# A table that fixes the whole order, and a short way for chunk 0's attention output, in a one-core adaLN transformer block

## The chip, the cores and the metric

One core of one Trainium2 chip runs the whole kernel in one launch. The metric is the device time of one execution in microseconds (us). Before the change it is 331.8 us, the median of three runs (331.46 to 332.3).

The engines are named as in the profile: PE is TensorE (matrix products, PEld its weight loads), DVE is VectorE, ACT is ScalarE, POOL is GpSimd. SP computes nothing and issues most of the DMA transfers, one after the other; a few are issued from ACT's queue. Each engine runs its own list of instructions strictly in the listed order, and an instruction that waits for a semaphore holds up everything listed behind it on that engine.

## The reference

```python
mod = (silu(c) @ w_mod)                       # six rows of 640: sa, ca, ga, sb, cb, gb
h = layernorm(x) * (1 + ca) + sa
x = x + ga * A(h)                             # A: attention, 32 heads of 20, sliding window of 256
h = layernorm(x) * (1 + cb) + sb
x = x + gb * B(h)                             # B: (sigmoid(h @ w_gate) * (h @ w_up)) @ w_down
# A(h): q, k, v = split(h @ wqkv);  o = softmax(mask(q k^T / sqrt(20))) v;  return o @ wo
```

x has 2048 rows of 640, wqkv is 640 x 1920, wo is 640 x 640, w_gate and w_up are 640 x 1536, w_down is 1536 x 640 and w_mod is 640 x 3840. Everything is bf16 outside PSUM.

## The kernel before

**Tiling.** The 2048 rows are cut into eight chunks of 256 (two blocks of 128 rows). For each chunk `a` the stages are: load of x, LayerNorm 1 (`ln_stats` on DVE, the power on POOL, the normalised rows `xh` on DVE or POOL), a turn to columns giving `hT`, the projections to q, k and v (`qkv`), a turn of q and k to `QT` and `KT`, scores (`score_set`), exponentials on ACT, masks on POOL, the product with v (`burst`), the division by the row sum (`norm`), the output projection with `wo` and the residual (`outproj`), LayerNorm 2, a turn giving `h2T`, and the gated MLP (`mlp`). The weights `wqkv`, `wo`, `wg`, `wu`, `wd` are loaded once and stay on chip. The gate rows ga and gb are multiplied into `wo` and `wd` ("wos", "wds" below) once they are computed in `mod_rows`, which sends them through a small DRAM buffer to all partitions (`gbc`).

**Two ways of turning.** The rows of chunks 0 to 2 (`NPH = 3`) and the q and k of chunks 0 and 1 (`NPQ = 2`) are turned on PE by products with `ident`, then copied out of PSUM. The later ones, and every `h2T`, are turned by DMA transposes issued on SP; `h2T` and the DMA-turned `hT` are then scaled and shifted in place (`modulate`).

**The way out of attention.** `norm` leaves `On`, a tile of 128 partitions holding four heads, each padded from 20 to 32 rows. Eight DMAs per chunk ("doc", 40 KB each) write the 20 used rows of each head to DRAM, and two DMAs read them back without the gaps as `oT`, five tiles of 128 rows, so that the output projection needs five passes (`NDT = 5`) per 128 x 320 result. For chunk 0 these DMAs are issued from ACT's queue (`OWE`), for the others from SP.

**Buffers that bound the order.** PSUM products use four banks in rotation (pool `M`); scores have one tile of four banks (`S`). Q and k that are turned by DMA pass through four staging buffers (`stg`), two per block of rows, which come free when the transposes have read them. Raw and normalised x of later chunks use four buffers (`x0`).

**What sets the order.** Nothing runs in the order in which it is written. `Prog.op` records each operation with its engines, a planner's cost, its dependences and its buffers; `schedule` is a list scheduler that walks time forward on those costs, and among the operations that could start next takes the one with the smallest priority from the table `PRIO` (line 408 on); `emit` then writes each engine's list with the semaphore waits. DMA transfers rotate over 24 semaphores, and each also waits for the one before it on the same semaphore.

**Lines of the profile.** Products are recorded by one helper, so all of full height have line 722 and those on parts of the array (scores, the product with v, the modulation rows) line 723; L703 and L714 are filler products that only keep PE running at the start; L880, L881 copy `hT` out, L916 and L917 copy the projections and turned tiles out, L1038 is the exponential, L1063 the mask, L1105 to L1114 `norm`, L1187 the residual, L847 and L848 `modulate`, L839 the DMA transposes, L623 and L624 all other DMAs.

Of the kernel before, what the change touches and what calls it, by code (L numbers as in the profile page):

```python
# [8 lines left out]
ALU = mybir.AluOpType  # L9
# [72 lines left out]
class Prog:  # L82
# [8 lines left out]
    def op(self, eng, fn, dur, reads=(), writes=(), prio=50.0, lat=0.05, work=None, tmin=0.0, extra=(), tag="", hold=(),  # L91
# [13 lines left out]
        o.prio = PRIO[self.seq] if self.seq < len(PRIO) else prio  # L105
# [46 lines left out]
    def schedule(self):  # L152
        free = {e: START for e in ENGS}
        bw = 0.0
        lastturn = False
        cand = {e: {} for e in ENGS}
# [6 lines left out]

        def arm(o):
            t = o.tmin
            for d in o.deps:
                t = max(t, d.end + (0.0 if (d.eng == "pe" and o.engs == ("pe",)) else d.lat))
            o.ready = t
            for e in o.engs:
                cand[e][o.seq] = o  # L170

        def slot_time(pool, s):
            ten = pool.tenant[s]
            if ten is None:
                if not all(x.done for x in pool.init[s]):
                    return None
                return max([x.end + x.lat for x in pool.init[s]], default=0.0)
            if ten.left:
                return None
            return max(x.end + x.lat for x in ten.rel)  # L180

        def slots_for(o):

            st = 0.0
            taken = {}
            got = []
            for t in o.tiles:
                if t.slot is None and t.mate is not None:
                    if any(g[0] is t for g in got):
                        continue  # L190
                    bs = None
                    for s in range(0, len(t.pool.tenant), 2):
                        ra, rb = slot_time(t.pool, s), slot_time(t.pool, s + 1)
                        if ra is not None and rb is not None and (bs is None or max(ra, rb) < bs[0]):
                            bs = (max(ra, rb), s)
                    if bs is None:
                        return None
                    got += [(t, bs[1] + t.odd), (t.mate, bs[1] + 1 - t.odd)]
                    st = max(st, bs[0])
                elif t.slot is None:  # L200
                    bs = None
                    used = taken.setdefault(t.pool, set())
                    for s in range(len(t.pool.tenant)):
                        if s in used:
                            continue
                        rt = slot_time(t.pool, s)
                        if rt is not None and (bs is None or rt < bs[0]):
                            bs = (rt, s)
                    if bs is None:
                        return None  # L210
                    used.add(bs[1])
                    got.append((t, bs[1]))
                    st = max(st, bs[0])
                else:
                    for x in t.prev:
                        st = max(st, x.end + x.lat)
            return st, got

        for o in self.ops:
            if o.nleft == 0:  # L220
                arm(o)
        n = len(self.ops)
        placed = 0
        while placed < n:
            best = None
            for e in ENGS:
                c = cand[e]
                if not c:
                    continue
                lst = []  # L230
                tmin = None
                for o in c.values():
                    st = max(free[e] + (SWITCH if e == "pe" and o.mode != pemode else 0.0), o.ready)
                    if e == "dve" and o.port:
                        st = max(st, free["pool"])
                    elif e == "pool":
                        st = max(st, portend)
                    if o.isdma and e == "sp":
                        st = max(st, bw - QMAX)
                    if o.tiles:  # L240
                        got = slots_for(o)
                        if got is None:
                            continue
                        st = max(st, got[0])
                    lst.append((st, o))
                    if tmin is None or st < tmin:
                        tmin = st
                if not lst:
                    continue
                eps = PE_EPS if e == "pe" else 0.04  # L250
                pick = min((x for x in lst if x[0] <= tmin + eps), key=lambda x: (x[1].prio, x[1].seq))
                key = pick[0]
                if e == "dve" and pick[1].port:
                    key = max(max(free[e], pick[1].ready) + PORTLAG, pick[0])
                if best is None or key < best[0]:
                    best = (key, e, pick[1], pick[0])
            if best is None:
                left = [(o.tag, o.engs, [t.pool.name for t in o.tiles if t.slot is None]) for e in ENGS
                        for o in cand[e].values()][:40]
                raise RuntimeError(f"no op can be placed: {placed} of {n}: {left}")  # L260
            _, e, o, st = best
            for x in o.engs:
                cand[x].pop(o.seq, None)
            o.eng = e
            for t, s in slots_for(o)[1]:
                ten = t.pool.tenant[s]
                t.prev = list(t.pool.init[s]) if ten is None else list(ten.rel)
                t.slot = s
                t.pool.tenant[s] = t
# [26 lines left out]
            placed += 1  # L296
# [12 lines left out]
            for x in o.succ:  # L309
                x.nleft -= 1  # L310
                if x.nleft == 0:
                    arm(x)
# [90 lines left out]
def c_pe(n):  # L403
# [128 lines left out]
LEAD = 2  # L532
# [14 lines left out]
def build(nc, A_x, A_wqkv, A_wo, B_x, B_w_gate, B_w_up, B_w_down, c, w_mod, out, S=2048):  # L547
# [131 lines left out]
    for i in range(4):  # L679
        load_w3(320 * i, 320 * i + 320, 1.12, 0.30 + 0.005 * i, "wq" if i < 2 else "wk", lat=-0.4)  # L680
# [648 lines left out]
```

## Time and profile before

| what | value |
|---|---|
| median of three runs | 331.8 us |
| the profiled execution, whole | 332.45 us |
| its span, first to last instruction | 330.7 us |
| mean granted TensorE clock | 0.995 |
| PE, DVE, ACT, POOL busy | 319.8, 213.3, 214.2, 186.9 us |
| products on PE | 4918 |
| bytes moved by DMA | 37.87 MB, mean 114 GB/s |

The span and the 1.75 us around it make up the profiled execution's time. Busy time of PE counts from the start of a product to its modelled end, so it includes the filler products at the start and products that ran at a lower clock.

Some durations that the steps need, each the mean of one instruction: a copy of 128 x 512 out of PSUM is 0.69 us on DVE and 0.60 us on ACT; the exponential of 128 x 1536 is 1.45 us; a mask of 128 x 1024 is 1.06 us on POOL; `norm` of half a chunk is two transposes of 0.69 us, a reciprocal of 0.35 us, a product of 0.83 us and a transpose of 1.23 us; the issue of one DMA transpose holds SP 1.24 us in quiet stretches and up to 4.4 us in busy ones.

### The profile page before, as it was taken

What the parts mean: (1) busy time and instruction counts of PE and PEld (TensorE: products, weight loads), DVE (VectorE), ACT (ScalarE), POOL (GpSimd) and SP (SyncE); (2) the same over time, 40 slices, a digit from 0 to 9 for tenths busy, and PEclk for the clock granted to TensorE, in tenths of its full rate; (3) what the DMA queues carried; (4) which work ended last, traced back from release to release, by engine and by line L of the source; (5) the groups of instructions that cost most, each with busy time, mean ns of one, the idle gap of its engine ahead of it and who ended that gap; (6) DMA issues with size and microseconds to landing.
All of it is one profiled execution on the core that took longest, in us unless ns stands there. A gap on an engine that the chain in (4) does not pass through costs nothing.

```text
span 330.7 us, 11708 instructions
## 1 busy us (share of the span) xinstructions
PE 319.8 (97%) x4918; PEld 224.0 (68%) x4918; DVE 213.3 (65%) x419; ACT 214.2 (65%) x319; POOL 186.9 (57%) x271
## 2 busy tenths in 40 slices
PE   7999888979999999999999999999999999999997
PEld 2664633535786658765777557877787788788885
DVE  5688888768979673676395748657645577273232
ACT  1598786788688687948787977794878673112120
POOL 3127868878898786657566847493747493011000
PEclk9999999979999999999999999999999999999999
DMA  7999799995523639205712484610411323202101
GB/s 267 374 363 350 121 327 264 165 231 94 107 68 76 113 88 151 60 18 96 137 23 59 85 119 76 117 46 5 116 44 24 97 48 36 65 22 42 42 0 42
DMA packets 71695, 37.87 MB, mean 114 GB/s; under 512 B 45274, under 2 KB 70362, under 8 KB 71642
## 3 DMA queue, kind: packets, MB, share of 16 engines
q1 hardware_dynamic: 67792, 33.67, 46.1%
q10 hardware_dynamic: 3850, 3.44, 3.3%
q8 instruction: 39, 0.64, 0.8%
q14 instruction: 14, 0.11, 0.1%
HBM read 21.30 MB, written 5.25 MB: 80 GB/s over the span
## 4 chain that ended last, share of the span: by engine, by line
PE 91%; DMA 4%; DVE 1%; ACT 1%; POOL 1%; issue 1%; ACTq 0%; POOLq 0%
PE M L722 74%; PE S L723 8%; PE M L723 7%; DMA QT<-stg 2%; PE S L703 2%; DMA hT<-x 1%; ACT E L1038 1%; PE S L722 0%; POOL E L1063 0%; DVE QT L917 0%; ACT hT L880 0%; POOL st L819 0%; DVE silubc L694 0%; PE S L714 0%; ACT hT L847 0%
## 5 line engine op out<-in xcount | busy, mean ns | idle before, releaser
L1038 ACT ACTIVATE E<-S 128x512 bf16<-128x512 f32 (+2 forms) x184 | 151.1, 878 | 44.6 <-PE S L723 42.4
L1063 POOL TENSOR_SCALAR_AFFINE_SELECT E<-E 128x512 bf16<-128x512 bf16 (+1 forms) x176 | 142.8, 837 | 62.4 <-ACT E L1038 61.6
L722 PE MATMUL M<-wqkv,hT 128*128 128x480 bf16 (+1 forms) x340 | 73.9, 361 | 3.6 <-DMA QT<-stg 1.2
L722 PE MATMUL M<-h2T,wu 128*128 128x256 bf16 x480 | 65.7, 273 | 0.0
L722 PE MATMUL M<-h2T,wg 128*128 128x256 bf16 x480 | 62.8, 273 | 0.0
L722 PE MATMUL M<-wd,hh 128*128 128x320 bf16 (+2 forms) x396 | 57.9, 295 | 0.0
L1232 ACT ACTIVATE sig<-M 128x512 f32<-128x512 f32 x48 | 28.8, 604 | 40.0 <-PE M L722 36.8
L1234 DVE SCALAR_TENSOR_TENSOR hh<-sig,M 128x512 bf16<-128x512 f32 x48 | 32.5, 678 | 32.5 <-PE M L722 16.0
L722 PEld LDWEIGHTS M<-wqkv,hT 128*128 128x128 bf16 x340 | 31.1, 99 | 32.6 <-issue 2.3
L722 PEld LDWEIGHTS M<-h2T,wg 128*128 128x128 bf16 x480 | 46.1, 98 | 7.4 <-issue 0.3
L722 PEld LDWEIGHTS M<-h2T,wu 128*128 128x128 bf16 x480 | 45.4, 98 | 7.9 <-issue 0.2
L722 PEld LDWEIGHTS M<-wd,hh 128*128 128x128 bf16 x396 | 37.1, 98 | 13.4
L1105 DVE STREAM_TRANSPOSE T<-M 128x512 f32<-128x512 f32 x32 | 21.2, 698 | 23.1 <-PE S L723 21.0
L723 PEld LDWEIGHTS S<-QT,KT 20*64 20x64 bf16 (+1 forms) x1856 | 19.9, 100 | 21.2 <-ACT E L1038 11.9
L723 PE MATMUL S<-QT,KT 20*64 20x256 bf16 (+5 forms) x1856 | 32.1, 228 | 1.5 <-ACT E L1038 1.0
L1253 DVE TENSOR_TENSOR x<-M,x 128x320 bf16<-128x320 f32 (+2 forms) x33 | 15.8, 477 | 26.7 <-PE M L722 26.4
L812 DVE BATCH_NORM_STATS2 st<-x 128x6 f32<-128x320 bf16 x64 | 28.3, 477 | 3.3 <-DMA x<-in_A_x_dram 3.1
L817 POOL TENSOR_SCALAR st<-st 128x2 f32<-128x2 f32 x16 | 4.5, 280 | 38.8 <-DVE st L814 38.5
L722 PE MATMUL M<-wo,oT 128*128 128x320 bf16 x160 | 25.0, 300 | 0.0
L723 PE MATMUL M<-E,V 128*32 128x128 bf16 (+1 forms) x960 | 22.7, 246 | 0.8 <-DVE hT L881 0.6
L917 DVE CAST stg<-M 128x480 bf16<-128x480 f32 (+1 forms) x25 | 14.6, 584 | 13.3 <-PE M L722 12.7
L723 PEld LDWEIGHTS M<-E,V 128*32 128x32 bf16 x960 | 19.2, 97 | 5.2 <-issue 4.4
(75 smaller groups left out, 252.5 us busy)
## 6 DMA issues: line engine op xcount, KB each, us to landing
x<-in_A_x_dram SPq DMA_DIRECT2D x17, 160.0 KB
doc<-On SPq DMA_DIRECT2D x56, 40.0 KB
wd<-in_w_mod_dram SPq DMA_DIRECT2D x6, 320.0 KB
wd<-in_B_w_down_dram SPq DMA_DIRECT2D x4, 480.0 KB
wqkv<-in_A_wqkv_dram SPq DMA_DIRECT2D x4, 400.0 KB
wu<-in_w_mod_dram SPq DMA_DIRECT2D x5, 320.0 KB
x<-in_A_x_dram ACTq DMA_DIRECT2D x9, 160.0 KB
oT<-doc SPq DMA_DIRECT2D x7, 192.0 KB
```

The source lines that it names most:

```text
L703: ins = e.matmul(p_S.aps[0][:, 3, :], Eall[:, 0, 0:128], Eall[:, 0, 128:640], start=True, stop=True)
L722: return e.matmul(o, l, r, start=st, stop=sp, skip_group_check=True)
L723: return e.matmul(o, l, r, start=st, stop=sp, tile_position=tp, skip_group_check=True)
L812: A("dve", lambda e, g, bi=bi, j=j: e.bn_stats(v(bi * 12 + j * 6, 6), src[bi].ap[:, j * 320:(j + 1) * 320]), 0.48, reads=[src[bi].r()], wr ...
L817: A("pool", lambda e, g: e.tensor_scalar(v(28, n), var(), EPS, None, op0=ALU.add), 0.2, reads=[st.r(("m", bi)) for bi in range(n)], writes ...
L917: return e.tensor_copy(dst(), src())
L1038: A("act", lambda e, eng: e.activation(dst(), src(), ACT.Exp, scale=SM_SCALE), c_act(n), reads=[Sp.r()], writes=[E.r(key)], prio=3, tag=f" ...
L1063: A("pool", lambda e, eng: e.affine_select(rows(dst), rows(src), pattern=[[0, 8], [sign, n]], compare_op=ALU.is_ge, fill=0.0, base=base, c ...
L1105: A("dve", lambda e, g, h=h: e.transpose(T1.ap[:, 512 * h:512 * h + 512], X[h].ap), 0.694, reads=[X[h].r()], writes=[T1.r(h)], prio=3.5, t ...
L1232: A("act", lambda e, g, pg=pg, sg=sg: e.activation(sg.ap[:], pg.ap[:], ACT.Tanh, scale=0.5), c_act(512), reads=[pg.r()], writes=[sg.r()], ...
L1234: A("dve", lambda e, g, pu=pu, sg=sg, f0=f0: e.scalar_tensor_tensor(out=hh.ap[:, f0:f0 + 2, :], in0=sg.ap[:].rearrange("p (a b) -> p a b", ...
L1253: A("dve", lambda e, g, ps=ps, bi=bi, c0=c0, n=n: e.tensor_tensor(x1[bi].ap[:, c0:c0 + n], ps.ap[:, 0:n], x1[bi].ap[:, c0:c0 + n], op=ALU. ...
```

## The change

**Order.** The list scheduler is gone. The table `PRIO` now has one number for each operation: operations are taken in the order of these numbers, and the number modulo 5 names the engine that runs it. Buffers are still given out by the planner's clock. Several planner costs and latencies are changed with it.

**Chunk 0's way out of attention.** Chunk 0 no longer goes through DRAM. `wo` is loaded a second time as `wop`, spread so that it matches the padded heads: 20 rows of weights, then 12 rows of zeros, for each of four heads, in eight tiles (`NG = 8`). `wop` lies in the memory of `hh` (so two of the modulation loads move from there to `wd`), is cleared by one DVE operation and filled by four DMAs of 20 partitions. The projection of chunk 0 multiplies `On` by `wop` directly, in eight passes instead of five. As `wop` has no gate in it, a DVE operation multiplies each product by `gbc` into a `sig` tile, and a second operation (on DVE or POOL) adds the residual. `wo` is gated for the later chunks as before. The MLP's gate row gets a tile of its own (`gbd`).

**Chunk 0's LN2 output** is turned on PE (`NPB = 1`), with scale and shift in the copies out of PSUM, in place of two DMA transposes and `modulate`.

**Loads.** `wm2`, `wo` and others have other places in SP's list; most x loads of the middle stage move from ACT's queue to SP's. By the built programs ACT's queue issues 8 DMAs where it issued 28, SP's 183 transfers and transposes become 195, and PE's list has 4940 products.

```diff
-        o.prio = PRIO[self.seq] if self.seq < len(PRIO) else prio
+        o.prio = PRIO[self.seq] if PRIO else prio
...
+        for o in sorted(self.ops, key=lambda x: x.prio):
+            assert all(d.done for d in o.deps), o.tag
+            e = ENGS[o.prio % 5]
+            assert e in o.engs, (o.tag, e)
+            o.eng = e
+            st = max([o.tmin, free[e] + (SWITCH if e == "pe" and o.mode != pemode else 0.0)]
+                     + [d.end + (0.0 if d.eng == "pe" and e == "pe" else d.lat) for d in o.deps])
...
-NPB = 0
+NPB = 1
...
-    gbc = sb("gbc", [128, D])
+    gbc, gbd = sb("gbc", [128, D]), sb("gbd", [128, D])
...
-             hhall[:, NDT * D:2 * NDT * D].rearrange("p (t f) -> p t f", t=NDT),
+             wd[:].rearrange("p a b -> p (a b)")[:, NDT * D:2 * NDT * D].rearrange("p (t f) -> p t f", t=NDT),
...
-    dma(lambda: wo[:], lambda: A_wo.rearrange("(t p) f -> p t f", p=128), 2.25, writes=[R_wo], prio=0.5, tag="wo")
-    load_bulk(wm_ap[2], wm_src[:, :, 2560:3200], Rm[2], 0.46, 0.6, "wm2", cuts=(3, 5))
+    R_wop = [R(f"wop{j}") for j in range(4)]
+    wop = hhall[:, 0:NG * D].rearrange("p (g f) -> p g f", g=NG)
+    o_wz = A(("dve", "pool"), lambda e, g: e.memset(hhall[:, 0:NG * D], 0.0), {"dve": 1.6, "pool": 4.7}, writes=R_wop, prio=1)
+    for j in range(4):
+        dma(lambda j=j: wop[32 * j:32 * j + DH], lambda j=j: A_wo.rearrange("(g j r) f -> j r g f", j=4, r=DH)[j], 0.56,
+            writes=[R_wop[j]], prio=0.5 + 0.01 * j, tag="wop", nonc=True)
...
         def close(q, X):
             On = Tile(p_On, f"On{a}_{q}")
             norm(X, On, a)
+            if not a:
+                Ons.append(On)
+                if q == 1:
+                    x1, h2 = outproj(a, Ons)
+                    mlp(a, x1, h2)
+                return
...
+                if not a:
+                    pairs = [(lambda t=t, bi=bi, half=half, ps=ps: (
+                        ps.ap[:, 0:320], oT[t // 4].ap[:, t % 4 * CH + bi * 128:t % 4 * CH + bi * 128 + 128], wop[:, t, half * 320:half * 320 + 320]))
+                        for t in range(NG)]
+                    o = pe_chain(ps, 320, pairs, [[oT[t // 4].r()] + R_wop for t in range(NG)], 15, f"wo{a}",
+                                 hold=[x1[bi]], gate=NG - 1, step=4)
...
+                    A("dve", lambda e, g, ps=ps, sg=sg, half=half: e.tensor_tensor(
+                        sg.ap[:, 0:320], ps.ap[:, 0:320], gbc[:, half * 320:half * 320 + 320], op=ALU.mult), c_dve(320),
+                      reads=[ps.r(), R_gbc], writes=[sg.r()], prio=4.5, tag="gate_0")
+                    A(("dve", "pool"), lambda e, g, sg=sg, bi=bi, half=half: e.tensor_tensor(
+                        x1[bi].ap[:, half * 320:half * 320 + 320], sg.ap[:, 0:320], x1[bi].ap[:, half * 320:half * 320 + 320],
+                        op=ALU.add), {"dve": c_dve(320), "pool": 0.56}, reads=[sg.r(), x1[bi].r()], writes=[x1[bi].r(("h", half))], prio=4.5, port=True, tag="res1_0")
+                    continue
```

More of the change, by code (lines that the diff above doesn't have):

```diff
@@ L162, in schedule @@
         portend = 0.0
[L164 to L170, printed above, removed]
+        freed = {}
         def slot_time(pool, s):
@@ L177, in slot_time @@
                 return max([x.end + x.lat for x in pool.init[s]], default=0.0)
[L178 to L186, printed above, removed]
-            for t in o.tiles:
[L188 to L269, printed above, removed]
@@ L308, in schedule @@
                     t.rel = list(last.values())
[L309 to L312, printed above, removed]
+                    freed[t] = max(x.end + x.lat for x in t.rel)
         self.order = order
@@ L809, in v, with part @@
             return st.ap[:, lo:lo + w]
+        def part(bi, j):
+            return [src[bi].r(("h", j))] if ("h", j) in src[bi].res else []
         for bi in range(n):
@@ L874, in pe_transposes @@
         prev = {}
-        for blocks, (dt, pv, rp) in [((bi,), x) for bi in range(2) for x in evs] if a == 0 else [((0, 1), x) for x in evs]:
+        for blocks, (dt, pv, rp) in [((bi,), x) for bi in range(2) for x in evs] if a == 0 and ln == "a" else [((0, 1), x) for x in evs]:
             lo, hi = blocks[0] * 128, blocks[-1] * 128 + 128
```

75 lines of the change are left out of this document (53 added, 22 removed), and 223 rows, old and new, of the table PRIO.

## The prediction

> **What bounds the kernel now.** I read the page's totals first, then PE in stretches, then PE's waits, then PE's timeline.
>
> ```profile
> PE 319.8 (97%) x4918; PEld 224.0 (68%) x4918; DVE 213.3 (65%) x419; ACT 214.2 (65%) x319; POOL 186.9 (57%) x271
> ...
> DMA  7999799995523639205712484610411323202101
> ```
>
> PE is busy for 97% of the span, so two things can shorten the kernel: fewer or faster products, and the 3% in which PE stands. DMA is near full for the first nine of 40 slices, so a load cannot be made earlier there without another becoming later.
>
> ```profile
> 0.00:10.00 10.00, 7.44 (x55) 1.00 0.83 284
> ...
> 30.00:40.00 10.00, 9.44 (x198) 1.00 0.84 201
> 40.00:50.00 10.00, 8.41 (x122) 1.00 1.20 288
> 50.00:60.00 10.00, 8.77 (x115) 1.00 1.08 255
> 60.00:70.00 10.00, 8.95 (x203) 1.00 0.99 190
> 70.00:80.00 10.00, 8.91 (x136) 0.83 0.85 162
> 80.00:90.00 10.00, 10.00 (x140) 1.00 0.54 91
> ```
>
> The columns are stretch, length, PE busy (products), granted clock, DMA share, GB/s. PE has no gap from 80 us until the end's tail. What can be won lies before 80 us: between 30 and 80 us PE is busy 44.48 of 50 us, so 5.52 us idle.
>
> ```profile
> PE M L722 <- DMA QT<-stg: 1.2, 1, 1.2
> PE M L722 <- ACT hT L847: 1.1, 1, 1.1
> PE S L723 <- ACT E L1038: 1.0, 1, 1.0
> PE M L722 <- DVE stg L917: 0.9, 1, 0.9
> PE M L723 <- DVE hT L881: 0.6, 1, 0.6
> PE S L723 <- DVE QT L917: 0.6, 1, 0.6
> ```
>
> No single cause: DMA transposes (QT; hT before its scaling), the exponential and copies out of PSUM each hold PE once. In common they have that PE's list at that place holds only projections of chunks 2 to 4, which share the staging buffers and the transposes; chunk 0's MLP (wg, wu) begins at 82.8 us, since its input goes through DRAM and two DMA transposes.
>
> ```profile
> 1.30 5.18 PE L703 MATMUL S<-E 128*128 128x512 bf16 x12 [1.30 <-DVE E L698]
> 6.41 0.17 PE L688 MATMUL M<-ident,oT 5*128 5x5 bf16 x1
> ...
> 8.52 0.45 PE L722 MATMUL S<-silubc,wd 128*128 128x64 bf16 x10 [1.26 <-DVE st L814]
> ...
> 12.29 2.20 PE L722 MATMUL M<-wqkv,hT 128*128 128x320 bf16 x15 [0.30 <-ACT hT L880]
> ...
> 71.07 3.87 PE L722 MATMUL M<-wqkv,hT 128*128 128x480 bf16 x10 [1.14 <-ACT hT L847]
> ...
> 75.23 2.20 PE L722 MATMUL M<-wqkv,hT 128*128 128x480 bf16 x10
> ```
>
> Two further losses. At 71.07 ten products take 3.87 us that take 2.20 us at 75.23: 1.67 us at a lower clock (0.83 in that stretch) after waits of 0.98 and 1.14 us within 2.6 us. And the start is a chain of waiting: the small product that turns c (L688) stands behind twelve fillers of 0.43 us, and from it follow silu(c), the modulation products at 8.52 and the first projection at 12.29 us.
>
> **The change, part by part.** The sum is made on the profiled execution, 332.45 us (span 330.7 and 1.75 around it), 0.65 above the median.
>
> *Start: -1.4 us.* In the new list the turning of c stands behind eight fillers: 1.30 + 8 x 0.43 = 4.74 instead of 6.41 us. DVE then has three LN statistics from 3.94 us (0.42 each), c, a fourth, silu, two aggregates (0.2 each) and the broadcast of 0.80 us: about 7.1 instead of 8.37 us. The six fillers left end near 7.1 too, so the modulation products start at about 7.25, 1.3 us earlier, and have one filler of 0.22 us less between them: 1.4 in all. The loads bear it: five loads of w_mod and two of x, 1.97 MB, stand ahead, and at the first slice's rate (267 GB/s over 8.3 us, 2.2 MB) they are in by 7.6 us; the first wqkv pieces follow. The added clearing of wop on DVE costs nothing where DVE waited for x, from 1.45 to 3.94 us: by the rows of the clearings (0.33 us for 320 elements, 0.21 for 192) 2560 elements are 2.4 us. Without that cover up to all 1.4 us go. Three clearings of staging buffers move to POOL, which stood idle 4.66 us before its first LN power at 8.58. Bounds: 0 (c lands only after 6.4 us, which the trace hides) to 2.0.
>
> *Added products: +2.2 us.* Eight passes instead of five for four results are 12 products of 128x320, at 0.137 us start to start (15 in 2.05 us): 1.64. Ten turns of LN2 rows at 0.058 us (four in 0.23): 0.58. Both are on PE's path. Upper bound from busy time by count: 12 x 0.156 (25.0 us / 160) + 10 x 0.114 (3.2 / 28) = 3.0. [...]
>
> *Middle stage: -7.2 us (5.52 idle and 1.67 of clock), and new waits of +2.5.* Eight doc transfers, two oT loads and two h2T transposes of chunk 0 go; a wop of 0.8 MB comes (2.3 us of DMA at 350 GB/s, issued by 35 us, mostly before the stage). ACT's queue issues 20 DMAs fewer; at 0.28 to 0.46 us each some ten of them lay between 35 and 55 us, among its exponentials. With chunk 0's MLP ready sooner, PE's list has it about 40 projection products (8.5 us) earlier, interleaved with chunk 4's projections, and V projections that need no staging buffer lie between q and k. So every wait listed above has other work in its place.
>
> What is late next: adding PE's new list up (0.213 us per 480 columns, 0.137 per 320, 0.36 per score set, 0.8 and 1.44 for products with v), from a first projection at 10.9 us, chunk 0's projection comes at 10.9 + 38.8 = 49.7 us. It needs the second half of `norm`, whose product with v ends at 42.3. DVE has statistics of chunks 4 and 5 listed ahead of it, and these wait for x loads that SP now issues behind two hT transposes. Before, those x loads were issued at 39.9 to 41.6 us and DVE got them at 44.5 and 47.5. SP passes the two transposes at 38.98 before; the loads that gate them are free some 3 us earlier now, so I put the last x load's issue at 38 and its landing at 43 to 44.5; norm and what DVE has between (a V copy 0.66, wos 0.9, gq and modt 0.65) take 4.9 + 2.2 us: 50 to 51.6, up to 2 us late. Behind that wait stand all of PE's products. Then gate (0.48), add (0.48 on DVE, 0.54 to 0.88 on POOL by its nearest rows), statistics, power (1.0), xh and copies (0.55 each) lie between chunk 0's last projection at 56.8 and its MLP at 64.3: they fill 6 to 7.5 us, 0 to 0.7 late. I take 2.5 for both and small others. Bounds: 0.5, and 7.2 if the stage idles as before. The gate and LN2 work on DVE (four products more, copies in place of in-place scaling) is otherwise hidden: DVE is busy 8 us in 10 there.
>
> [...] In this trace 2.1 us in two pieces cost 1.67 us, and 1.19 us at 55 us nothing; by the costlier row 1.7 us would be added.
>
> *After 80 us: 0.* No wait before; every product stays. Up to +1.5 if the new order waits where the old did not. The tail keeps its form (a last piece of 192 columns instead of 128: +0.1).
>
> Sum: 332.45 - 1.4 + 2.2 - 7.2 + 2.5 = 328.55; less 0.65 for the median, 327.9, say 328.0.
>
> **The rivals.**
>
> *All waits go* (new waits 0.5): 326.0. For it: each part has work in its place. Against: the norm chain above has no slack. Chance 0.15.
>
> *The stage idles as before* (new waits 5 to 7): 330.4 to 332.4, about 331.5. For it: DMA stays full until 80 us with no fewer bytes, and the transposes take their 4 to 8 us whatever the order. Against: the staged projections lie further apart. Chance 0.17.
>
> *Slower: the x loads come late enough to stop norm.* If SP passes the two hT transposes no earlier than now (39 us), the last x load lands at about 47, norm ends at 54, chunk 0's projection waits 4.3 us; meanwhile the two PSUM banks of its product with v stay taken, so that the V projections of chunk 3 wait too; MLP 0 shifts as well (1.5) and the clock falls (1.7): 7.5 us and no gain at the start: 331.8 + 2.2 - 7.2 + 7.5 = 334.3 with 0, 332.9 with the start's 1.4. It decides once norm's input stage on DVE (L1105's successor) starts after 46 us. For it: DVE waited 0.25 and 0.96 us for just these loads. Against: their gates come earlier. Chance 0.15.
>
> That the order changes nothing is excluded: the list has the eight-pass products and no doc transfer of chunk 0.
>
> **How the numbers follow.** Forecast 0.53 (328.0, own range 325.8 to 330.3), rivals 0.15, 0.17, 0.15. A measurement of this kernel can tell about 0.3% (1 us) from no change. Faster than 330.8: 0.53 and 0.15, and a quarter of the third case, 0.04: 0.72. Within 330.8 to 332.8: most of the rest of the third, 0.12. Slower: 0.16. The range of 8 in 10 runs from 325.0 to 333.2: it leaves out the tail of the first rival and most of the slower one beyond.
>
> **What would show it.** The first projection near 10.9 us instead of 12.29; PE idle between 30 and 80 us near 2.5 us instead of 5.5, its clock 1.00 in every stretch; MLP 0 (wg) from about 65 to 68 us instead of 82.8; the largest PE wait just before the products of On with wop, released by DVE; x landing on DVE before 45 us. Wrong if PE waits for DMA as long as before, if a gap appears after 80 us, or if the first projection is not earlier.

## The result, and the profile after

| | before | after |
|---|---|---|
| median of runs (lowest to highest) | 331.88 us (331.46 to 332.3) | 337.02 us (335.52 to 339.63) |
| ratio, with its 95% interval | | 1.0149 [1.0109, 1.0188] |
| profiled execution, whole / span | 332.45 / 330.7 us | 335.52 / 333.8 us |
| first projection, first MLP product | 12.29, 82.8 us | 11.52, 73.9 us |
| PE idle from 30 to 80 us | 5.52 us | 5.09 us |
| mean granted clock | 0.995 (profiled execution) | 0.985 to 0.995, run by run |

The changed kernel is 1.5% slower. Here and below, a run more than 1.5% above the fastest of its kernel is left out of the ratio (two of again's ten, one of xslot's four, three of wopearly's twelve), while medians and ranges count every run. In the page of after the totals differ little:

```profile
PE 322.5 (97%) x4939; PEld 225.2 (67%) x4940; DVE 207.9 (62%) x412; ACT 219.2 (66%) x328; POOL 183.3 (55%) x274
```

PE in stretches (start and end, length, PE busy, products, granted clock, DMA share, GB/s) shows where the expected gain is not:

```profile
0.00:10.00 10.00, 7.42 (x69) 1.00 0.80 256
...
30.00:40.00 10.00, 8.90 (x149) 1.00 1.15 245
40.00:50.00 10.00, 8.51 (x153) 1.00 0.89 227
50.00:60.00 10.00, 9.93 (x156) 1.00 0.97 215
60.00:70.00 10.00, 7.68 (x171) 1.00 1.10 255
70.00:80.00 10.00, 9.89 (x110) 0.83 0.92 196
80.00:90.00 10.00, 10.00 (x176) 1.00 0.55 148
```

From 30 to 80 us PE still stands 1.10 + 1.49 + 0.07 + 2.32 + 0.11 = 5.09 us, and one stretch has the clock of 0.83 again. The waits are other ones (wait, total us, times, longest):

```profile
PE S L671 <- issue: 1.9, 1, 1.9
PE M L670 <- DVE T L1058: 1.5, 1, 1.5
PE S L651 <- DVE E L646: 1.3, 1, 1.3
PE S L670 <- DVE x L785: 1.2, 1, 1.2
PE M L671 <- DMA wu<-in_w_mod_dram: 0.9, 1, 0.9
```

Two of them are the case: one of 1.5 us for T, which is `norm`'s first step, and one of 1.9 us that the profile puts down to nothing ("issue"). PE's timeline (start, length, operation, count, in brackets the idle time before it) has them at 49.20 and 69.95 us:

```profile
49.20 0.58 PE L670 MATMUL M<-wqkv,hT 128*128 128x480 bf16 x2 [1.48 <-DVE T L1058]
...
67.64 0.38 PE L671 MATMUL S<-QT,KT 20*128 20x64 bf16 x28 [0.29 <-ACT E L991]
69.95 0.21 PE L671 MATMUL S<-QT,KT 20*128 20x64 bf16 x4 [1.93 <-issue]
```

The first is a V projection that needs the PSUM bank in which the product with v waits for `norm`. The second stands in the middle of a set of 32 equal products, between the 28th and the 29th, where no operand can be missing.

The chain of work that ended last (start, length, what) leads back from the first of them:

```profile
32.01 7.45 DMA hT<-x
...
39.53 0.33 SPq L568
...
40.38 4.99 DMA x<-in_A_x_dram
45.39 1.28 DVE st L765 x3
...
48.52 0.63 DVE T L1058
```

SP issues chunk 3's two transposes of x at 32.01 us. The next x tile in SP's list goes into a buffer which these transposes still read; SP therefore stands until they have landed, at 39.5 us. The three x loads follow at 39.53, 40.38 and 41.30, and DVE has statistics of chunks 4 and 5 ahead of `norm`: it starts T at 48.44 us.

### The profile page after: what moved, and what is told of

Same layout as the page of the kernel before. It is cut to its first block, busy times and chain, and to the rows that moved or that the text cites. A ratio compares the mean times of both kernels' runs of the same rounds, so it can differ in the third digit from the quotient of the medians.

```text
span 333.8 us, 11744 instructions
## 1 busy us (share of the span) xinstructions
PE 322.5 (97%) x4939; PEld 225.2 (67%) x4940; DVE 207.9 (62%) x412; ACT 219.2 (66%) x328; POOL 183.3 (55%) x274
## 4 chain that ended last, share of the span: by engine, by line
PE 82%; DMA 6%; SPq 3%; ACT 3%; POOL 2%; issue 2%; DVE 1%; POOLq 0%; ACTq 0%
PE M L670 69%; PE S L671 8%; PE M L671 6%; SPq L568 3%; DMA wqkv<-in_A_wqkv_dram 2%; ACT E L991 2%; DMA hT<-x 2%; DMA x<-in_A_x_dram 1%; POOL E L1016 1%; DVE st L765 1%; ACT hT L800 1%; POOL st L772 0%; POOL x L782 0%; DVE stg L870 0%; DVE T L1058 0%
## 5 line engine op out<-in xcount | busy, mean ns | idle before, releaser
L1016 POOL TENSOR_SCALAR_AFFINE_SELECT E<-E 128x512 bf16<-128x512 bf16 (+1 forms) x176 | 141.0, 829 | 68.8 <-ACT E L991 63.8
L670 PE MATMUL M<-wqkv,hT 128*128 128x480 bf16 (+1 forms) x340 | 75.8, 358 | 2.0 <-DVE T L1058 1.5
L670 PE MATMUL M<-h2T,wu 128*128 128x256 bf16 x480 | 70.6, 273 | 0.0
L670 PE MATMUL M<-h2T,wg 128*128 128x256 bf16 x480 | 67.5, 273 | 0.0
L670 PE MATMUL M<-wo,oT 128*128 128x320 bf16 x140 | 23.1, 300 | 0.0
L1067 DVE STREAM_TRANSPOSE On<-Tn 128x1024 bf16<-128x1024 bf16 x16 | 19.7, 1232 | 0.2
```

Source lines behind the costliest of these rows:

```text
L670: return e.matmul(o, l, r, start=st, stop=sp, skip_group_check=True)
L1016: A("pool", lambda e, eng: e.affine_select(rows(dst), rows(src), pattern=[[0, 8], [sign, n]], compare_op=ALU.is_ge, fill=0.0, base=base, c ...
L1067: A("dve", lambda e, g: e.transpose(On.ap[:], Tn.ap[:]), 1.22, reads=[Tn.r()], writes=[On.r()], prio=4, tag=f"tr2_{a}")
```

## Experiments

Whole lists would be long, so an edit of the order is shown as the engine's list with names: `x8` to `x11` are loads of x (128 rows each), `wg0`, `wu1` and so on the first and later parts of those weights, `wop` one of the four transfers of the spread copy, `T3` chunk 3's transposes of x. Ratios are to the kernel before, run on the same chip beside them. The runs are spread over several chips; kernels of different chips, wide and after among them, are compared by these ratios alone.

### The changed kernel again, and the first explanation: the x loads and norm

> The changed kernel as it is, a second profile of it. Theory A (late tiles of x): the statistics of chunks 4 and 5 hold VectorE again, the second norm of chunk 0 starts at 48 us or later and TensorE waits 1.2 to 1.8 us for its first transposes. Theory B (instruction supply): the gap of 1.93 us that no semaphore explains need not come back at the same place; if it is TensorE waiting for its own instructions it should appear here too, somewhere between 60 and 75 us, with one instruction packet late beside it. If the gap is absent and the time is still above 334 us, B explains little. Time 335 to 339 us by both.

Measured: 337.28 us (334.09 to 341.12), 1.0126 [1.0086, 1.0165]. The wait for T (1.6 us) and the gap behind the 28th of 32 products (1.6) are there again; idle from 30 to 80 us is 5.26 us. So neither is a chance of one execution.

```diff
 x9 gets the buffer that chunk 2's rows have left; SP:
-T3 wg0 x9 wop x8 wu0 x11
+T3 wg0 x8 x9 wop wu0 x11
```

> Tile 9 of x goes into the buffer that chunk 2's turned rows left, and is issued behind tile 8, so SP no longer stands until the transposes of chunk 3 have landed (it stood from 36.2 to 39.5 us). Theory A: tiles 8 and 9 are issued at 37 to 38 us and land by 43.5, VectorE waits under 0.5 us for x, the second norm of chunk 0 starts by 47, TensorE's wait of 1.48 us for it goes to under 0.4, and the time falls by 1.5 to 3 us. Theory B: the time moves by less than 1 us unless the unexplained gap of 1.9 us goes by chance. Rival C (the transfer queues are full anyway): the tiles land as late as before, 44.5 to 45.5, whatever the issue time, and nothing changes.

Measured: 338.13 us, 1.0124 [1.0049, 1.0198]. The first x load is issued at 36.09 us instead of 39.5, but DVE gets its data only at 43.76 us (after: 44.35), norm starts at 47.36 and PE waits 1.9 us for T. SP's stand was a symptom: issued 3.4 us earlier, the load was used only 0.6 us sooner.

```diff
 DVE:
-statistics of chunks 4 and 5 ... norm (second half of chunk 0)
+norm (second half of chunk 0) ... statistics of chunks 4 and 5
```

> On VectorE the second norm of chunk 0 (two input transposes, reciprocal, division, output transpose, with the one small modulation add they need) goes ahead of the statistics of chunks 4 and 5. All else is as in the changed kernel. Theory A: the input transposes start as soon as the product with v is done, at 45.5 to 46 us instead of 48.4, the wait of 1.48 us on TensorE goes, the first projection of chunk 0 starts by 52 instead of 54.7, and the time falls by 1.5 to 3 us. If the statistics are late instead, the transposes of chunk 4 and its projections pay: a new TensorE wait behind 75 us of up to 2 us. Theory B: the gap of 1.9 us near 68 us stays and with it most of the loss.

> Both edits together. Theory A: as the better of the two alone, 333 to 334.5 us, no more, because they remove one and the same wait. Theory B: what is left above 332 us is the unexplained gap and the low clock behind it, about 3.5 us together where it occurs.

Measured: 337.65 us, 1.0156 [1.0075, 1.0237], and with both edits 338.76 us, 1.0176 [1.0122, 1.023]. The waits of PE in the first:

```profile
PE M L829 <- DVE V L1029: 3.3, 1, 3.3
PE S L830 <- ACT E L1150: 1.9, 3, 1.4
PE M L830 <- POOL E L1175: 1.8, 2, 1.2
...
PE S L830 <- issue: 0.2, 1, 0.2
```

No wait for T is left, and the time is no better: the copy of V out of PSUM, the exponentials and POOL's masks hold PE instead. The copy of V is late by the edit itself, since DVE now has the statistics ahead of it. The masks stand on POOL behind the scaling of chunk 3's `hT`, which needs the same transposes; these land later still here, and the scaling starts at 41.89 us instead of 40.21. The exponentials are late because one x load is left in ACT's own queue: it is issued at 41.79 us, and ACT computes nothing for 3.12 us around it. So the test is not a clean one, but taking the wait for T away gained nothing, and the late transposes stand ahead of two of the three new waits.

### What lies ahead of the transposes

The added loads are the suspect. The next kernel keeps the order and takes the bytes of the copy away (64 columns of one row are left of each transfer), so that chunk 0's output projection multiplies almost only by zeros:

```diff
-wop[32 * j:32 * j + DH], A_wo.rearrange("(g j r) f -> j r g f", j=4, r=DH)[j]
+wop[32 * j:32 * j + 1, 0, 0:64], A_wo.rearrange("(g j r) f -> j r g f", j=4, r=DH)[j, 0:1, 0, 0:64]
```

> The four loads of the second copy of w_o (0.8 MB) shrink to 64 columns of one row each, so chunk 0's projection is left out in effect (its products run on zeros); every instruction stays. Theory C (transfers of the stage up to 80 us are the bound, and the copy adds to them): tiles 8 and 9 of x land 1.5 to 3 us earlier, the wait for the second norm shrinks from 1.5 us to under 0.6, the w_mod wait at 37 us goes, and the time falls by 2 to 3 us. Theory A (only SP's standing order matters): under 1 us, since x is issued as late as before. Theory B: the unexplained gap of 1.6 to 1.9 us behind the 28th of 32 score products stays.

Measured: 333.01 us (332.01 to 333.95), 1.0027 [0.9999, 1.0055]. The x load behind the transposes is issued at 36.25 us, and the wait for T is gone. But two gaps of the other kind stand there:

```profile
50.41 0.58 PE L670 MATMUL M<-wqkv,hT 128*128 128x480 bf16 x2 [1.18 <-issue]
68.09 0.24 PE L671 MATMUL S<-QT,KT 20*128 20x64 bf16 x4 [2.49 <-issue]
```

So most of the loss comes from the copy's loads, and the gap has another cause.

```diff
 SP:
-T3 wg0 x9 wop x8 wu0 x11 gate wg0
+T3 x8 x9 wop x11 gate wg0 wg0 wu0
```

> Behind chunk 3's transposes SP issues tiles 8, 9 and 11 of x and the last quarter of the copy first, and only then the halves of w_gate and w_up (1.7 MB) that stood ahead of them; tile 9 takes the buffer that chunk 2 left. Moving the issue alone by 3.4 us brought the landing only 1.6 us forward (43.8 instead of 45.4), because 0.58 MB of w_gate was ahead in the queue. Theory C: x lands by 41.5, the statistics of chunks 4 and 5 are done before the product with v is (45.5), TensorE's wait for the second norm goes to under 0.3 us and the time falls by 1.5 to 2.5 us, unless w_gate or w_up is now late at 74 us. Theory B: the gap near 68 us stays.

Measured: 335.57 us, 1.011 [1.005, 1.017]. The transposes land still later, at about 41.5 us; the wait for T goes, but waits for exponentials (2.2 us), a modulation load at the start (1.9), masks (1.2) and two gaps (1.9, 1.2) come. Here too ACT stands at its x load:

```profile
41.42 0.37 ACTq L726 DMA_DIRECT2D x<-in_A_x_dram  x1
41.85 0.60 ACT L1149 ACTIVATE E<-S 128x512 bf16<-128x512 f32 x1 [2.69 <-issue]
```

This change of places, behind the transposes, is no cure.

### The gap in the middle of equal products

The page of after has 39 packets of 16 KB in a queue named "instruction":

```profile
q8 instruction: 39, 0.64, 0.8%
```

PE's products and weight loads are 4939 + 4940 instructions, 253 to a packet; by this count alone the author took the packets for blocks of PE's own instructions. The transfers in short windows show such a packet at 53.9 us and the next only at 67.6 us, 13.7 us later; in the kernel before, the packets between 16 and 86 us come 6 to 11 us apart. (One earlier interval in after is as long, 26.8 to 41.1 us, and leaves no gap.) From 61.2 to 63.3 us SP issues four loads of weights, 1.7 MB. The theory: PE's next block of instructions stands behind them.

The traces show this beside it. Such gaps stand in after, again, xslot, norm, nowop, nowspread, xfirst, woback, wobspread3 and wide, 13 in all, from 0.2 us (norm) to 2.6 (woback). In the timelines of after, again, nowop, nowspread and wide they stand at only two places of PE's list, behind the 28th of the 32 products and inside the V projection shown for nowop. Between the two lie 252 products (nowop), with their weight loads 504 instructions or, at 253 each, two packets. In after PE goes on 2.3 us after a packet has started (67.6 and 69.95 us), in wide 2.5 us (63.84 and 66.33). Two edits test what makes the packet late; one moves two of the loads, the other cuts five filler products at the start into 19 pieces, so that by the theory a block ends 14 products earlier.

```diff
 SP:
-... wd wg1 wd wu1 ... q and k transposes of chunk 3
+... wd wd ... q and k transposes of chunk 3, wg1 wu1
```

> Two of the four bulk loads that SP issues in one burst at 61 to 63 us (0.77 MB of w_gate and w_up, first needed near 85 us) go behind the four query and key transposes of chunk 3. Theory B (TensorE waits for a block of its own instructions, which stands in the transfer engines behind the burst): the block comes earlier and the gap behind the 28th product shrinks from 1.6-1.9 us to under 0.7; with it the low clock that can follow it; 1 to 3 us off the time. If the gap is not from transfers it stays at 1.6 to 1.9 us.

Measured: 334.64 us (333.21 to 336.15), 1.0068 [1.0043, 1.0093]. The gap is gone, the packet comes at 65.8 us, and the wait for T (1.8 us) stays.

```profile
68.68 0.41 PE L829 MATMUL S<-QT,KT 20*128 20x64 bf16 x32 [0.29 <-ACT E L1149]
```

```diff
-ins = e.matmul(p_S.aps[0][:, 3, :], Eall[:, 0, 0:128], Eall[:, 0, 128:640], start=True, stop=True)
+cut = (0, 512) if k or i > 4 else (0, 128, 256, 512) if i == 4 else (0, 128, 256, 384, 512)
+for a, b in zip(cut, cut[1:]):
+    ins = e.matmul(p_S.aps[0][:, 3, a:b], Eall[:, 0, 0:128], Eall[:, 0, 128 + a:128 + b], start=True, stop=True)
```

> Five warm-up products at the start are cut into 19 pieces with the same columns in all: 14 products more, 28 instructions, no work added. Theory B: if the gap is TensorE at the end of a fetched block of instructions, it moves with the count and comes behind the 14th of the 32 score products instead of the 28th, 1.5 to 2 us long as before. If it hangs on the data or on a buffer it stays behind the 28th. Time as the changed kernel, 335 to 339 us.

Measured: 335.06 us (333.79 to 336.88), 1.0081 [1.0051, 1.011].

```profile
68.80 0.41 PE L673 MATMUL S<-QT,KT 20*128 20x64 bf16 x32 [1.23 <-ACT E L993]
```

The gap does not move to the 14th product, as was expected: it is gone, the packet comes at 62.0 us, ahead of the loads' bulk, and waits for exponentials (2.2 us in all) come instead. So the gap goes when loads are moved (spread), and also when 14 products are added at the start with no load moved (shift). When PE asks for a packet no trace shows. In shift the packet started with 132 products to go to the place of the gap, in spread with 62, in after with 28. That the loads hold it up fits, but is not shown: each edit also shifts other waits, and the gap's size follows from no formula here.

### Both causes removed

```diff
 SP's list of spread, with this too:
-wop[32 * j:32 * j + DH], A_wo.rearrange("(g j r) f -> j r g f", j=4, r=DH)[j]
+wop[32 * j:32 * j + 1, 0, 0:64], A_wo.rearrange("(g j r) f -> j r g f", j=4, r=DH)[j, 0:1, 0, 0:64]
```

> Two edits that were run alone, together: the second copy of w_o is not loaded (chunk 0's projection left out in effect, every instruction kept), and the 0.77 MB of w_gate and w_up go behind chunk 3's transposes. Theory B+C (the loss is transfers: the added copy, and blocks of TensorE's instructions that stand behind bulk loads): the gap of 2.5 us that was left near 68 us goes too; 330 to 331.5 us, the time at which the prediction's sum would arrive without the new waits. If the sum itself was wrong (the added products and turns cost far more than 2.2 us), the time stays at 332.5 to 333.5.

Measured: 331.08 us (329.46 to 332.24), 0.9977 [0.9948, 1.0006], with the clock at 1.0 in all ten runs. PE in stretches:

```profile
30.00:40.00 10.00, 9.78 (x152) 1.00 0.94 253
40.00:50.00 10.00, 8.82 (x185) 1.00 0.88 190
50.00:60.00 10.00, 9.97 (x125) 1.00 0.99 181
60.00:70.00 10.00, 8.60 (x182) 1.00 1.25 235
70.00:80.00 10.00, 10.00 (x117) 1.00 0.93 252
```

Idle from 30 to 80 us is 2.83 us, near the 2.5 us that the prediction gave as the mark of success; the first projection starts at 10.85 us (forecast 10.9), and MLP 0 at 68.81 us (forecast 65 to 68). Without the copy's bytes and with these loads moved, the order does what the forecast pictured, but the time is still 3 us above it. Two gaps that the profile puts down to "issue" are left, 1.21 and 0.57 us.

### Bytes, or the form of the transfers

If it is the bytes, moving others of the same number should do as well. First the load of `wo` (0.82 MB), issued at 13.1 us in after, was put later, with one part of `wg1` moved too; then with all of `wg1` and a part of `wu1` behind the transposes; then with the edits of xslot and shift on top:

```diff
 SP (wolate; wospread has the lower line in place of the upper one's second part):
-... wo ... last load of wm1 ... wg1 ... x11 ... q and k transposes of chunk 3
+... last load of wm1, wo ... x11 wg1 ... q and k transposes of chunk 3
+... last load of wm1, wo ... x11 ... q and k transposes of chunk 3, wg1 wg1 wu1
```

> Nothing left out. The first copy of w_o (0.8 MB, needed from 51 us) is issued behind w_mod's last piece of the gate instead of ahead of the copy, and 0.58 MB of w_gate (needed at 85 us) behind tile 11 of x instead of at 23 us. Theory C: w_mod's piece lands before TensorE asks for it (wait of 0.5 to 0.9 us at 37 gone), the tiles of x up to 11 are not delayed by those 1.4 MB, and 0.5 to 2 us are won, less than the 4.2 us that came from not loading the copy at all, since the bytes stay. Theory A: no change over 0.5 us. Theory B: the gap near 68 us stays or grows.

> Nothing left out. w_o's first copy later as in the run with it alone, and three bulk loads (1.34 MB of w_gate and w_up, needed from 85 us) behind chunk 3's transposes. Theory B+C: both gains, 332.5 to 334.5 us; if the three loads now hold up the tiles of x of chunks 6 and 7 behind them, a wait shows on VectorE at 85 to 95 us.

> The run before it with two edits more: tile 9 of x in the buffer that chunk 2 left, issued behind tile 8, and 14 products more from cutting five warm-up products, which moves the ends of the instruction blocks by 28 instructions. Theory B+C: 332 to 334 us; the wait for the second norm under 1 us and no unexplained gap over 0.7 us before 80 us. By the prediction's sum nothing under 330 is to be had.

Measured: 337.9 us, 1.0184 [1.0117, 1.0252]; 335.13 us, 1.0109 [1.0062, 1.0157]; 338.42 us, 1.0198 [1.0149, 1.0246]. All missed. In the first the transposes land later still, at about 42.4 us, ACT's x load waits for them, and exponentials hold PE for 4.8 us in all. Then `wo` was moved out of the stage altogether, to 81 us (its scaling to 94 to 98 us), with nothing left out (the next three add the moves of spread, of spread with the first part of `wg1` too, and of spread and shift):

```diff
 SP:
-... wo wop ... x14 ...
+... wop ... x14 wo ...
 DVE: the five scalings of wo from the middle stage to 94 to 98 us
```

> Nothing left out. The first copy of w_o, which chunk 1's projection reads first at 101 us, is loaded at 81 instead of 13 us, and VectorE scales it by the gate at 94 to 98 us (in gaps of 1.3 and 2.7 us) instead of at 52 to 63. The second copy stays. Theory C (bytes in a full stage): as not loading the second copy, 332.5 to 334 us, wait for the second norm and for w_mod at 37 us under 0.5 us each. Rival (the copy's place in SP's queue, or its narrow form of 20 partitions): 336 to 338 us as the changed kernel. A new wait of TensorE on VectorE at 96 to 104 us of up to 1 us would speak against the place chosen.

> The same, and 0.77 MB of w_gate and w_up behind chunk 3's transposes. Theory B+C: as the run that left the copy out and had this edit, 330.5 to 332 us, with no clock loss, so level with the kernel before (331.8) or just under it. If B was chance, 332.5 to 334 us.

> The same, and also the first part of w_gate's second half (0.58 MB, loaded at 23 us, needed at 85) behind those transposes. Theory C: transposes and x land earlier again, up to 0.5 us more; but 1.34 MB then stand ahead of the tiles of x of chunks 6 and 7 and of w_o, and VectorE waits for them at 85 to 95 us. 330 to 333 us.

> As the second, with the 14 products more at the start that move the block ends by 28 instructions. Theory B: the two unexplained gaps that were left there (1.2 us near 50, 0.6 us near 66) hang on when a block is asked for, so they may go or come back elsewhere; by their size 0 to 1.8 us less, 329.5 to 331.5 us.

Measured: 338.11 us, 1.0184 [1.0132, 1.0236]; 335.83 us, 1.01 [1.006, 1.0139]; 335.64 us, 1.0103 [1.0066, 1.0141]; 336.7 us, 1.0136 [1.0102, 1.017]. With 0.82 MB less ahead the x load behind the transposes is issued at 39.97 us, as late as before; with 0.58 MB less again (the third) at 39.00. In the first no byte at all is moved from 21.0 to 22.4 us (0 GB/s). Bytes ahead of the transposes, in this amount, are not the cause.

What stays is how the copy's transfers are made: each writes 20 partitions. One kernel keeps their places and their 0.82 MB and writes all 128 partitions, so that chunk 0's projection multiplies by the wrong rows of `w_o`:

```diff
-wop[32 * j:32 * j + DH], A_wo.rearrange("(g j r) f -> j r g f", j=4, r=DH)[j]
+wop[:, j:j + 1 + j // 3], A_wo.rearrange("(t p) f -> p t f", p=128)[:, j:j + 1 + j // 3]
```

> The four transfers of the second copy keep their places in SP's queue and their 0.82 MB in all, but each writes 128 partitions (plain tiles of w_o) instead of 20, so chunk 0's projection reads wrong rows. Theory D (form): chunk 3's transposes land at 36 to 37.5 us instead of 39.5 to 40.5, tile 9 of x is issued by 37.5, and the time falls to 333 to 335 us. Theory E (place): as the changed kernel, transposes at 39 us or later and 336 to 338.5 us. [...]

Measured: 331.19 us (329.95 to 333.51), 0.9991 [0.9962, 1.002], clock 1.0 in all ten runs. The transfers of after from 28 to 40 us, then those of this kernel from 28 to 37 us (GB/s in 40 slices of 0.3 and 0.225 us; the last lines have issues and the median us to landing):

```profile
GB/s 355 306 316 343 371 334 346 376 243 179 213 218 184 179 205 256 294 376 388 397 380 393 364 353 328 312 261 112 120 124 120 115 119 67 49 102 280 284 396 251
...
hh<-in_A_wo_dram SPq DMA_DIRECT2D x2, 200.0 KB
...
hT<-x SPq DMA_TRANSPOSE x2, 7.4
```

```profile
GB/s 283 280 347 347 347 387 410 376 415 448 398 387 358 376 432 398 364 393 427 381 387 404 393 429 347 348 355 320 265 222 168 122 82 64 49 222 288 275 376 362
...
hh<-in_A_wo_dram SPq DMA_DIRECT2D x1, 320.0 KB
...
hT<-x SPq DMA_TRANSPOSE x2, 5.3
```

In after the rate drops from some 350 to between 179 and 256 GB/s from 30.4 to 32.8 us, in the wide kernel it stays near 400. The transpose whose landing the trace shows lands 5.3 us after its issue instead of 7.4, and the last part in after shows a plateau at 112 to 124 GB/s for 1.8 us that the wide kernel lacks. (The page of before shows no landing. POOL's scaling, which needs the transposes, gives a common measure: in before it starts 5.2 us after their first issue at 35.39, in wide 6.4, in after 8.2.)

```profile
40.58 2.71 POOL L848 TENSOR_SCALAR hT<-hT,mA 128x256 bf16<-128x256 bf16 x5 [0.76 <-DMA hT<-x]
...
37.74 1.67 POOL L801 TENSOR_SCALAR hT<-hT,mA 128x256 bf16<-128x256 bf16 x2
...
40.21 1.09 POOL L801 TENSOR_SCALAR hT<-hT,mA 128x256 bf16<-128x256 bf16 x2 [1.76 <-DMA hT<-x]
```

These are before, wide and after. SP of the wide kernel goes on at 36.73 us:

```profile
31.31 3.21 SPq L792 DMA_TRANSPOSE hT<-x  x2
34.57 0.59 SPq L568 DMA_DIRECT2D wg<-in_B_w_gate_dram  x1
36.73 0.34 SPq L568 DMA_DIRECT2D x<-in_A_x_dram  x1
```

The same bytes at the same places cost 5 us less (ratios 0.9991 against 1.0126 to 1.0149), though a gap of 1.54 us is left. So it is the form of the transfers that costs. Which part of the form is not separated: wide also cuts the copy into pieces of 160, 160, 160 and 320 KB and reads whole tiles of `w_o` in the order of its rows. The rate and the landings above go with the form; why the narrow one is slower no view here shows.

Last, the whole computation: the four narrow transfers where `wo` stood at 13 us, far ahead of the transposes, `wo` at 81 us, and the list of spread.

```diff
 SP:
-... wo wop ... wop ... wop T3 wg0 x9 wop ... wd wg1 wd wu1 ... 
+... wop wop wop wop ... T3 wg0 x9 ... wd wd ... wg1 wu1 ... wo
```

> Nothing left out, form unchanged. All four transfers of the copy are issued at 13 to 15 us, where the first copy of w_o stood (that one goes to 81 us, its scalings to 94-98, as in the runs before), ahead of the stretch in which SP stands until 21.8 us and the engines run dry; 0.77 MB of w_gate and w_up go behind chunk 3's transposes. Theory E (place): nothing of the copy stands ahead of chunk 3's transposes any more, they land by 37 us, the wait for the second norm is under 1 us, 331 to 333 us, as the run without the copy and with this edit (331.1). [...]

Measured: 331.9 us (330.16 to 336.4), 1.0008 [0.9983, 1.0032]. It differs from wobspread (1.01) only by the place of the four narrow transfers, so a place far ahead of the transposes helps as the wide form does. By the ratio it is level with the kernel before, and the best complete version of the new form; no complete version beats the kernel before. No profile of it is read here.

## Why the prediction was wrong, step by step

**The direction and the size were missed.** 328.0 us was forecast, range 325.0 to 333.2; 337.02 came. The step that failed is the one on the middle stage: "-7.2 us (5.52 idle and 1.67 of clock), and new waits of +2.5". Of the 5.52 us, 5.09 (after) and 5.26 (again) came back as other waits, and in after the clock's loss stayed too (0.83 from 70 to 80 us, 1.7 us). The new waits, taken as 2.5 with bounds 0.5 and 7.2, thus came to 5.3 us in again and 6.8 in after, the second near the upper bound. Within the step, the last x load was put at 38 us and was issued at 41.3, because the first of them needs a buffer that the transposes still read.

**Why.** The copy of `w_o` was costed by its bytes, "2.3 us of DMA at 350 GB/s, issued by 35 us, mostly before the stage". Its bytes are harmless (wide), its narrow form ahead of the transposes is not. And the second price was in no term: PE stood up to 2.6 us (woback) in a gap that the profile puts down to "issue", with the operands of its next product all there, and in after and wide it went on 2.3 and 2.5 us after a 16 KB packet of the "instruction" queue had started, a queue that stands in the same DMA profile as the loads. On the medians' ratios, wide takes away some 5 us, nowop 4, spread 2, nowspread 5; the effects overlap and do not add up.

**The rivals.** The slower rival's mechanism is what happened first: T started at 48.44 us, past the point of 46 us it named, the last x load was issued at 41.3 and the transposes landed at 39.5. Its price, 4.3 us at chunk 0's projection, came as 1.5 us at a V projection behind the held PSUM bank, which it had named too. But the x loads are not the remedy: neither xslot nor norm gains. The forecast gave this case 0.15.

**Start, -1.4 us.** 0.77 us in the profile of after (11.52), 1.04 in that of again (11.25), 1.44 in nowspread (10.85). The list bears the forecast, the loads do not always:

```profile
7.96 0.76 PE L670 MATMUL S<-silubc,wd 128*128 128x64 bf16 x20 [1.20 <-DVE x L785]
...
7.72 0.76 PE L670 MATMUL S<-silubc,wd 128*128 128x64 bf16 x20 [1.52 <-DMA wd<-in_w_mod_dram]
```

These are after and again. The turn of c starts at 4.83 us in after (forecast 4.74) and silu(c) is spread by 6.67, but the modulation products start at 7.96 and 7.72 us instead of 7.25. The page of again names a load of w_mod. That of after names a DVE step whose result these products do not read, so a load is the likelier cause there too. Right in direction; in after half the size.

**Added products, +2.2 us.** PE's busy time without clock losses went from 319.8 - 1.67 = 318.1 us to 320.9 in again, whose clock was 1.0: 2.8 us. The term was 0.6 us too small, inside its bound of 3.0. Busy time also holds the fillers, so this is a coarse reading. The list summed for the middle stage was short too: 38.8 us from the first projection to chunk 0's, where PE is busy 39.64 us in nowspread and 40.05 in after.

**After 80 us, 0.** 0.38 and 0.06 us of idle time from 100 to 120 us; inside the bound.

**The balance.** Again's profiled execution is 332.45 - 1.67 + 2.8 + 0.5 (idle of the whole span 11.4 instead of 10.9 us) = 334.1, and 334.09 was measured: with busy and idle time as its parts, this is a split of the difference, no proof. The median lies 3 us above it. Most runs of again have a granted clock of 0.985 to 0.995; at 3.4 us of half clock each (below) that would be one to three such stretches, 1.7 to 5 us, an estimate that fits, but no profile of these runs was read. With the copy's bytes gone and the loads moved the time is still 331.1 us and not 328.0: nowspread's PE is busy 321.5 us, 3.4 more than before without its clock loss, and gaps of 1.2 and 0.6 us remain. What else this kernel loses against the forecast is open.

**The clock.** The sum adds nothing for the clock behind the new waits: that waits of this length leave it alone was the author's estimate, and the runs do not bear it out throughout. In again, with waits of up to 1.6 us, the clock stayed at 1.0. In after it fell behind a gap of 1.93 us (0.83 from 70 to 80 us), in spread from 50 to 60 us (0.83) behind one of 1.79. Nor does the length of a gap alone decide: wolate has a wait of 3.0 us, and the granted clock of that execution is 1.0. Seen closely, the low clock of after is 0.50 for 3.4 us:

```profile
70.30:73.70 3.40, 3.29 (x37) 0.50 0.95 207
```

In before it is 0.50 from 71.08 to 74.50 us. In the 3.41 us just ahead of the low clock PE was busy for 1.29 us in before (67.67 to 71.08, 62% idle) and for 1.19 in after (66.85 to 70.26, 65%). From 46.40 to 49.80 us in after it was busy for 1.91 of 3.40 us (44% idle), and the clock stayed at 1.00 from 40 to 60 us. This is read off afterwards from two traces; no run moved a gap to test what makes the clock fall.

## What to carry to other kernels

A load was here not only its bytes: with the same bytes at the same places, its form decided how late the transposes queued behind it landed (5.3 us after their issue in wide, 7.4 in after) and 5 us of the time. The copy to 20 partitions had to go far ahead of the transposes that something waits for (wopearly, 1.0008), or into a wide form (wide, 0.9991). A wait that disappears only pays if the thing ahead of it does too: follow the chain back to the transfer that is late, and test it by changing its form before its place. When PE stands in the middle of equal products with nothing to wait for, look at the queue of instructions and at the loads just ahead, as for the gap of 1.93 us in after.

## What was not expected of the hardware

- With transfers of 200 KB to 20 partitions under way the rate fell from some 350 to between 179 and 256 GB/s for 2.4 us in after, and a transpose behind them landed 7.4 us after its issue, against 5.3 in wide.
- PE stood in gaps of 0.2 to 2.6 us (norm, woback) with nothing that the profile shows to wait for, at two places of its list; in after and wide the one behind the 28th of 32 equal products ended 2.3 and 2.5 us after a 16 KB packet of the "instruction" queue had started. It is gone in spread and wobspread, where 0.77 MB of loads are moved, and in shift; it is smaller with the loads moved in nowspread (0.57) and wobspread3 (1.0). What the packets hold, and that PE waited for one, is the author's reading of 39 packets for 9879 instructions and of these times.
- PE's clock fell to 0.50 for 3.4 us behind a gap of 1.93 us (after), to a mean of 0.83 from 50 to 60 us behind one of 1.79 (spread), and not behind a wait of 3.0 (wolate, granted clock 1.0).
- An x load issued 3.4 us earlier was used only 0.6 us sooner (xslot: issued at 36.09, used at 43.76 us; after: 39.5 and 44.35).
